# Transposing transfers out of SBUF and row factors by block transpose in a two-branch token mixer

## The chip, the cores and the metric

The kernel runs on one core of a Trainium2 chip. The metric is device time in microseconds (us) of one execution. TensorE (PE) multiplies matrices and can also transpose through an identity matrix; VectorE (DVE), ScalarE (ACT) and GpSimd (POOL) do elementwise work; SyncE (SP) issues nearly all transfers, in one queue, in program order. SBUF is the on-chip memory of 128 partitions, PSUM the accumulator memory that PE writes, DRAM the memory off the core.

## The reference, cut to what matters

S is 2048 rows, D is 512 columns, F is 1376; everything is bf16 in and out.

```python
xn = layernorm(x)                      # no gain or bias
# branch A: sliding dilated attention, 32 heads of 16, window of 8 rows 2 apart
q, k, v = split(xn @ wqkv)
o = softmax(q . k[s - 2*w]) . v[s - 2*w]   # per head, w = 0..7, masked before row 0
s = o @ wo
# branch B: shifted mixer and MLP on the same xn
h  = gelu(layernorm(xn) @ w1)          # a second layernorm of an already normed row
hs = [h0 one row later, h1 one row earlier, h2 two later, h3 two earlier] @ w2
x1 = xn + hs
h2 = gelu(layernorm(x1) @ w3) @ w4
out = x + s * silu(x1 + h2)
```

The second layernorm of a row that is already normed only multiplies it by a factor near one. This is the row factor below.

## The kernel before, in words

Rows are split into even rows (p = 0) and odd rows (p = 1), 1024 each, and these into four chunks of 512 rows: chunks 0 and 1 are even, 2 and 3 are odd. A chunk has four tiles of 128 rows. The order of the work is written out by hand: every instruction goes through `pin`, which keeps each engine's instructions in program order, and waits come from data dependencies alone. Transfers complete on eight counters in rotation, so that a transfer also waits for the one issued eight before it.

The first half of the program (to about 112 us) makes the operands, the second half (18 rounds of attention blocks, with the w4 products and the output products between them) uses them. In the first half, a chunk goes through these steps:

- `Norm.stats`, `root` and `apply` (L219 to L240) norm the rows in place in `xn`: statistics and apply on DVE, the root on POOL (on ACT for chunk 0).
- `turn` (L296) transposes two tiles on PE into a PSUM bank, and DVE copies them (L303) to `xnT`, the transposed rows. Chunk 0's first two tiles go one by one through `turn_one` (L307), which is copied out by ACT (L313).
- `rows2` (L248) makes the row factors, one column of 128 for each tile. The factors are needed along the free dimension, the same in all partitions. `rows2_spread` (L264, chunks 1 and 2) transposes them on PE (L266), copies them on DVE (L268), writes them to DRAM as `r2_d` (L269) and reads them back to all partitions into the last quarter of `xn2T` (L271). `rows2_here` (L273, chunks 0 and 3) spreads them with a product by ones on PE (L282) instead, copied out by ACT (L284) or DVE (L286).
- `scaled` (L288) multiplies `xnT` by the factors into `xn2T` on DVE.
- `q_all`, `k_all`, `v_pair` and `w1` multiply `xnT` or `xn2T` by weights on PE, each as halves of 8 products of 128x512. A half fills one bank of a pair of PSUM banks; there are three pairs in rotation (`pair`, L91). ACT empties them: q by L339, k twice by L354 (even and odd heads), v by L373, w1 by L400 with the gelu.
- `w2` (L415) multiplies the shifted rows of `hT`, DVE adds to `xn` (L435) and takes statistics; `columns` (L443) norms into `xn3`, writes the chunk to `x1n_dram` (L446) and reads it back transposed as `x1nT` by one transposing transfer of 512x512 (L450). `w3` (L459) multiplies it (L469) into `h3a` and `h3b`.

The values v are written to DRAM (`v_d`, L377) for the second half. The weights w3 and w4 are loaded at L545 and L574, between the steps of chunks 1 and 2. The part of the order that the change touches is, before:

```python
w1(0, 0); rows2_spread(1); load w3; turn(1, 0); turn(1, 1); w1(0, 1)
l2 stats, root, apply; rows2(2); l3 stats, root
scaled(1); q_all(1); k_all(1); v_pair(0, 4); l3.apply; rows2(3); v_pair(0, 6)
rows2_spread(2); w1(1, 0); turn(2, 0); turn(2, 1); w1(1, 1)
scaled(2); q_all(2); turn(3, 0); turn(3, 1); k_all(2); load w4
rows2_here(3); scaled(3); w1(2, 0); w1(2, 1); w1(3, 0); w1(3, 1); w2(0); columns(0)
```

Of the kernel before, what the change touches and what calls it, by code (L numbers as in the profile page):

```python
# [8 lines left out]
AF = mybir.ActivationFunctionType  # L9
ALU = mybir.AluOpType  # L10
BF16 = mybir.dt.bfloat16
# [3 lines left out]
def ap_of(base, dims, off=0):  # L15

    return bass.AP(base.tensor, base.offset + off, dims)
# [3 lines left out]
def kernel(  # L21
# [32 lines left out]
    CH = 512  # L54
    NCH = S // CH
    TPC = CH // P
# [22 lines left out]
    dram = ctx.enter_context(tc.tile_pool(name="dram", bufs=1, space=bass.MemoryType.DRAM))  # L79
# [8 lines left out]
    PS = psp.tile([P, 8, CH], F32, name="PS")  # L88
# [21 lines left out]
    wv_sb = b4([P, ND, D], "wv_sb")  # L110
    load_x(0, 0, 1)
    load_x(0, 1, 1)
    pin(SP.dma_start(out=wv_sb, in_=wqkv_v[:, :, 2 * D : 3 * D]))
    load_x(0, 2, 1)
    load_x(0, 3, 1)
    pin(SP.dma_start(out=wqk_sb[:, :, 0:D], in_=wqkv_v[:, :, 0:D]))
# [9 lines left out]
    w3_sb = wpl.tile([P, WS], BF16, name="w3_sb", tag="w")[:, 0 : ND * F].rearrange("p (dt f) -> p dt f", f=F)  # L126
# [11 lines left out]
    pin(DVE.memset(eps_t[:], EPS))  # L138

    for i in range(10):  # L140
        pin(PE.matmul(
            PS[:, 6 + i % 2, :], lhsT=ones_bf[:], rhs=ones_bf.unsqueeze(1).to_broadcast([P, TPC, P]),
            start=True, stop=True,
        ))

# [7 lines left out]
    m57 = const.tile([P, QB], BF16, name="m57")  # L153
    e_sb = const.tile([P, 8, 8, 16], BF16, name="e_sb")
    zero = const.tile([P, D], BF16, name="zero")

    def head_masks():
        pin(DVE.tensor_reduce(
# [36 lines left out]
    hT = [b8([P, ND, M + 2], f"hT{p}") for p in range(2)]  # L195
    kM = [kbp.tile([P, ND, MK, 2], BF16, name=f"kM{p}", tag="kM") for p in range(2)]
    v_d = [dram.tile([MK, 2, D], BF16, name=f"v_d{p}") for p in range(2)]
    r2_d = dram.tile([NCH, CH], BF16, name="r2_d")
    x1n_dram = dram.tile([S, D], BF16, name="x1n_dram")
    vst = [b4([P, 2, 2, D], f"vst{i}") for i in range(2)]  # L200


# [4 lines left out]
    def small_t(name, shape, dt=F32):  # L207
        return small.tile(shape, dt, name=name, tag=name)
# [37 lines left out]
    xn2Ts, r2s = {}, {}  # L246

    def rows2(c, ln):  # L248

        r2 = small_t("r2", [P, TPC])  # L250
        r2b = small_t("r2b", [P, TPC], BF16)
        eng = DVE if c == 0 else POOL
        pin(eng.tensor_tensor(out=r2, in0=ln.rstd, in1=ln.rstd, op=ALU.mult))
        pin(eng.tensor_tensor(out=r2, in0=r2, in1=ln.mv[:, :, 1], op=ALU.mult))
        if c == 0:
            pin(ACT.activation(r2, r2, AF.Sqrt, bias=eps_t[:]))
            with nc.allow_low_precision("bf16 row factors"):
                pin(DVE.reciprocal(out=r2b, in_=r2))
        else:
            rsqrt_eps(r2, r2)  # L260
            pin(POOL.tensor_copy(out=r2b, in_=r2))
        r2s[c] = r2b

    def rows2_spread(c):  # L264
        pt = single().bitcast(BF16)[0:TPC, 0:P]
        pin(PE.transpose(pt, r2s[c], ident[:]))  # L266
        t = small_t("r2t", [TPC, P], BF16)
        pin(DVE.tensor_copy(out=t, in_=pt))  # L268
        pin(SP.dma_start(out=r2_d[c].rearrange("(j q) -> j q", q=P), in_=t))  # L269
        xn2Ts[c] = b4([P, ND, CH], "xn2T")  # L270
        pin(SP.dma_start(out=xn2Ts[c][:, ND - 1, :], in_=r2_d[c : c + 1, :].to_broadcast([P, CH])))  # L271

    def rows2_here(c):  # L273
# [9 lines left out]
        if c == 0:  # L283
            pin(ACT.activation(t[:, ND - 1, :], pt, AF.Copy))  # L284
        else:
            pin(DVE.tensor_copy(out=t[:, ND - 1, :], in_=pt))  # L286

    def scaled(c):  # L288
        p, k = c // 2, c % 2
        t = xn2Ts[c]  # L290
        pin(DVE.tensor_tensor(
            out=t, in0=xnT[p][:, :, k * CH : (k + 1) * CH],
            in1=t[:, ND - 1, :].unsqueeze(1).to_broadcast([P, ND, CH]), op=ALU.mult,
        ))

    def turn(c, h):  # L296
        p, k = c // 2, c % 2
        i = k * TPC + 2 * h
        pt = single().bitcast(BF16).rearrange("p (a j q) -> p a j q", a=ND, j=2)
        for j in range(2):  # L300
            for dt in range(ND):
                pin(PE.transpose(pt[:, dt, j, :], xn[p][:, i + j, dt * P : (dt + 1) * P], ident[:]))  # L302
        pin(DVE.tensor_copy(  # L303
            out=xnT[p][:, :, i * P : (i + 2) * P], in_=pt.rearrange("p a j q -> p a (j q)")
        ))

    def turn_one(c, t):  # L307
        p, k = c // 2, c % 2
        i = k * TPC + t
        pt = single().bitcast(BF16)[:, 0 : ND * P].rearrange("p (a q) -> p a q", a=ND)  # L310
        for dt in range(ND):
            pin(PE.transpose(pt[:, dt, :], xn[p][:, i, dt * P : (dt + 1) * P], ident[:]))
        pin(ACT.activation(xnT[p][:, :, i * P : (i + 1) * P], pt, AF.Copy))  # L313

    def q_half(pts, lo, hi, nts=range(ND)):
        for nt in nts:
# [28 lines left out]
    def k_pad(p):  # L345
        pin(POOL.memset(kM[p][:, :, 0:8, :], 0.0))
        pin(POOL.memset(kM[p][:, :, M + 8 : MK, :], 0.0))

    def k_all(c, parts=(0, 1)):
        p, k = c // 2, c % 2  # L350
        for a in parts:
            pt = proj(c, a, wqk_sb[:, :, D : 2 * D], chunk(xnT, c))
            for e in range(2):
                pin(ACT.activation(  # L354
                    kM[p][:, 2 * a : 2 * a + 2, 8 + k * CH : 8 + (k + 1) * CH, e], pt, AF.Copy, scale=em[:, e : e + 1]
                ))
# [86 lines left out]
    def columns(c):  # L443
        ln = ln2[c]
        ln.apply(0, TPC)
        pin(SP.dma_start(  # L446
            out=x1n_dram[c * CH : (c + 1) * CH, :].rearrange("(i q) d -> q i d", q=P), in_=ln.dst
        ))
        x1nT = b4([P, ND, CH], "x1nT")
        pin(SP.dma_start_transpose(out=x1nT, in_=x1n_dram[c * CH : (c + 1) * CH, :]))  # L450
        x1nTs[c] = x1nT

    h3a, h3b = {}, {}
# [39 lines left out]
    pin(POOL.memset(zero, 0.0))  # L493
    k_pad(0)
    k_pad(1)
    pin(ACT.activation(
# [8 lines left out]
    for t in range(2):  # L505
        l0.root_act(t, t + 1, 1)
        l0.apply(t, t + 1)
    turn_one(0, 0)
    turn_one(0, 1)
    pv = pair()  # L510
    for t in range(2):
        v_mm(0, t, pv[:, t, :])
# [16 lines left out]
    for a in range(2):  # L529
# [10 lines left out]
    v_pair(0, 2)  # L540
    k_all(0, (1,))
    v_pad(0)
    w1(0, 0)
    rows2_spread(1)
    pin(SP.dma_start(out=w3_sb, in_=B_w3.rearrange("(dt q) f -> q dt f", q=P)))  # L545
    turn(1, 0)
    turn(1, 1)
    w1(0, 1)
    l2 = Norm(x_of(2), x_of(2), TPC, "l1")
    l2.stats(0, 4)  # L550
    l2.root()
    l2.apply(0, 4)
    rows2(2, l2)
    l3 = Norm(x_of(3), x_of(3), TPC, "l1")
    l3.stats(0, 4)
    l3.root()
    scaled(1)
    q_all(1)
    k_all(1)
    v_pair(0, 4)  # L560
    l3.apply(0, 4)
    rows2(3, l3)
    v_pair(0, 6)
    rows2_spread(2)
    w1(1, 0)
    turn(2, 0)
    turn(2, 1)
    w1(1, 1)
    scaled(2)
    q_all(2)  # L570
    turn(3, 0)
    turn(3, 1)
    k_all(2)
    pin(SP.dma_start(  # L574
        out=w4_sb[:, 0 : NF - 1, :],
        in_=B_w4[0 : (NF - 1) * P, :].rearrange("(ft q) n -> q ft n", q=P),
    ))
    pin(SP.dma_start(out=w4_sb[0:FL, NF - 1, :], in_=B_w4[(NF - 1) * P : F, :]))
    rows2_here(3)
    scaled(3)  # L580
    w1(2, 0)
    w1(2, 1)
    w1(3, 0)
    w1(3, 1)
    w2(0)
    columns(0)
    v_pad(1)
    q_all(3)
# [403 lines left out]
```

## Time and profile before

| what | us |
|---|---|
| median of 3 runs | 199.26 |
| lowest and highest of them | 197.72, 199.69 |
| the profiled execution's own time | 197.26 |
| its span, first to last instruction | 195.5 |
| PE busy in the span | 185.5 (95%) |
| ACT busy | 133.3 (68%) |
| DVE busy | 117.8 (60%) |
| POOL busy | 19.1 (10%) |
| mean granted TensorE clock | 0.996 |

The profile is of one execution. A group is the instructions of one line and engine on the same tiles, with their number, busy time and mean; the waits say what ended the idle time ahead of an instruction; the chain of waits is followed back from the last instruction and shows what set the end; the timeline lists instructions in order of time, merged where they follow each other, as start, length, engine, line, operation and number. PEld is the weight load ahead of a product, SPq the issue of a transfer on SP. A product of 128x512 is shown with 379 ns, and follows the one before it after some 216 ns, since products overlap.

### The profile page before, as it was taken

To read this page: it belongs to the slowest core of one execution; us is meant where nothing else is said; L and a number is where in the kernel's file an instruction comes from. 1 tells how busy PE (TensorE), PEld (TensorE's weight loads), DVE (VectorE), ACT (ScalarE), POOL (GpSimd) and SP (SyncE) were. 2 spreads that over 40 slices of the span, in tenths; PEclk is the share of its full clock that TensorE was granted. 3 is DMA by queue.
4 is the path that set the end of the run, shared out by engine and by line. 5 is a ranking of instruction groups with operands and counts; after the bars stand their busy time and mean duration, and the time that the engine had idled before them with its cause. 6 is when DMAs were issued, how large, how long until landed. Compare 5 with 4: busy or idle time off the path is not lost.

```text
span 195.5 us, 5255 instructions
## 1 busy us (share of the span) xinstructions
PE 185.5 (95%) x2253; PEld 91.8 (47%) x2283; DVE 117.8 (60%) x229; ACT 133.3 (68%) x151; POOL 19.1 (10%) x57
## 2 busy tenths in 40 slices
PE   7899999999999999999999999999999999999990
PEld 2474544554444444444444444445444544554540
DVE  5785767236076697494200035556487888798894
ACT  7399769649817615435656588877887876887871
POOL 3006066100002022006000000000000000000000
PEclk9999999999999999999999999999999999999998
DMA  4997480654000433752480051457565556582523
GB/s 131 339 368 239 132 282 15 218 158 157 0 0 3 136 83 109 215 107 65 110 260 0 0 162 60 157 166 232 153 216 161 137 155 215 127 247 51 171 91 126
DMA packets 33576, 28.12 MB, mean 144 GB/s; under 512 B 10760, under 2 KB 32528, under 8 KB 33552
## 3 DMA queue, kind: packets, MB, share of 16 engines
q1 hardware_dynamic: 33408, 27.71, 47.2%
q8 instruction: 18, 0.29, 0.6%
q10 hardware_dynamic: 144, 0.07, 0.1%
q14 instruction: 6, 0.05, 0.1%
HBM read 17.01 MB, written 8.67 MB: 131 GB/s over the span
## 4 chain that ended last, share of the span: by engine, by line
PE 85%; DMA 5%; DVE 4%; issue 2%; SPq 1%; ACT 1%
PE PS L469 19%; PE PS L328 19%; PE PS L764 19%; PE PS L427 5%; PE PS L811 4%; PE PS L795 4%; PE PS L652 3%; DMA wqk_sb<-in_A_wqkv_dram 3%; PE PS L626 3%; PE PS L362 3%; DMA x1nT<-x1n_dram 2%; PE PS L318 2%; PE PS L662 2%; PE PS L302 2%; DVE sg L825 2%
## 5 line engine op out<-in xcount | busy, mean ns | idle before, releaser
L469 PE MATMUL PS<-x1nT,w_sb 128*128 128x512 bf16 (+1 forms) x173 | 38.2, 379 | 0.4 <-DMA x1nT<-x1n_dram 0.3
L633 ACT ACTIVATE prob<-PS 128x1824 bf16<-128x1824 f32 x18 | 30.4, 1688 | 4.4 <-PE PS L626 3.6
L764 PE MATMUL PS<-w_sb,h3a 128*128 128x512 bf16 x112 | 29.2, 379 | 1.9 <-issue 1.7
L475 ACT ACTIVATE h3a<-PS 128x1024 bf16<-128x1024 f32 x16 | 16.4, 1024 | 21.0 <-PE PS L469 19.1
L777 DVE TENSOR_TENSOR xn<-PS,xn 128x512 bf16<-128x512 f32 x15 | 10.3, 686 | 32.0 <-PE PS L764 31.8
L469 PEld LDWEIGHTS <-w_sb 128*128 128x128 bf16 (+1 forms) x176 | 17.5, 100 | 20.9 <-issue 0.7
L328 PE MATMUL PS<-xnT,wqk_sb 128*128 128x512 bf16 x109 | 25.0, 379 | 0.2
L354 ACT ACTIVATE kM<-PS,em 128x1024 bf16<-128x1024 f32 x16 | 20.8, 1404 | 3.2 <-PE PS L328 3.2
L638 DVE TENSOR_TENSOR prob<-prob,maskb 128x1824 bf16<-128x1824 bf16 x18 | 19.8, 1102 | 1.8 <-ACT prob L633 1.8
L764 PEld LDWEIGHTS <-h3a 128*128 128x128 bf16 x128 | 11.3, 97 | 13.4 <-issue 1.2
L328 PEld LDWEIGHTS <-wqk_sb 128*128 128x128 bf16 x112 | 10.9, 98 | 12.8
L435 DVE TENSOR_TENSOR xn<-PS,xn 128x1024 bf16<-128x1024 f32 x8 | 9.6, 1213 | 11.3 <-PE PS L427 11.3
L811 PE MATMUL PS<-wo_sb,oT 128*128 128x512 bf16 (+1 forms) x68 | 15.5, 366 | 0.0
L328 PE MATMUL PS<-xn2T,w_sb 128*128 128x512 bf16 x62 | 14.6, 379 | 0.1
L427 PE MATMUL PS<-w_sb,hT 128*128 128x512 bf16 x63 | 14.4, 379 | 0.1
L821 ACT ACTIVATE sg<-PS 128x512 bf16<-128x512 f32 (+1 forms) x17 | 9.6, 572 | 6.1 <-PE PS L811 6.1
L764 PE MATMUL PS<-w_sb,h3b 128*128 128x512 bf16 (+1 forms) x44 | 12.8, 380 | 0.8 <-issue 0.8
L339 ACT ACTIVATE qT<-PS 128x1024 bf16<-128x1024 f32 x8 | 8.1, 1024 | 7.6 <-PE PS L328 7.6
L373 ACT ACTIVATE vst<-PS 128x512 bf16<-128x512 f32 (+1 forms) x12 | 8.8, 743 | 3.5 <-ACT sig L784 2.3
L221 DVE BATCH_NORM_STATS2 l1s<-xn 128x6 f32<-128x512 bf16 x16 | 10.1, 680 | 1.6 <-DMA xn<-in_A_x_dram 1.6
L400 ACT ACTIVATE hT<-PS 128x1024 bf16<-128x1024 f32 x8 | 8.1, 1031 | 3.8 <-PE PS L328 3.8
L221 DVE BATCH_NORM_STATS2 l3s<-xn 128x6 f32<-128x512 bf16 x16 | 10.2, 682 | 0.2
(105 smaller groups left out, 229.2 us busy)
## 6 DMA issues: line engine op xcount, KB each, us to landing
ring<-v_d SPq DMA_DIRECT2D x18, 256.0 KB, 3.3
v_d<-vst SPq DMA_DIRECT2D x16, 256.0 KB, 2.7
x1n_dram<-xn SPq DMA_DIRECT2D x4, 512.0 KB
xo<-in_A_x_dram SPq DMA_DIRECT2D x8, 256.0 KB, 4.1
ring<-rec_d SPq DMA_DIRECT2D x4, 456.0 KB, 4.7
out_dram<-xo SPq DMA_DIRECT2D x7, 256.0 KB
xn<-in_A_x_dram SPq DMA_DIRECT2D x6, 256.0 KB, 7.9
w_sb<-in_B_w_dram SPq DMA_DIRECT2D x1, 1376.0 KB
```

The source lines that it names most:

```text
L221: pin(DVE.bn_stats(out=self.st[:, j, :], in_=self.src[:, j, :]))
L328: pin(PE.matmul(pt[:, b, :], lhsT=w[:, dt, nt * P : (nt + 1) * P], rhs=rhs[:, dt, :], start=(dt == 0), stop=(dt == ND - 1),))
L354: pin(ACT.activation(kM[p][:, 2 * a : 2 * a + 2, 8 + k * CH : 8 + (k + 1) * CH, e], pt, AF.Copy, scale=em[:, e : e + 1]))
L427: pin(PE.matmul(pt[:, j, :], lhsT=w2_src(p, g, m0), rhs=w2_sb[:, g, :], start=(g == 0), stop=(g == ND - 1),))
L435: pin(DVE.tensor_tensor(out=xs, in0=pts[h], in1=xs, op=ALU.add))
L469: pin(PE.matmul(pt[:fs, ft % 2, :], lhsT=w3_sb[:, dt, ft * P : ft * P + fs], rhs=x1nT[:, dt, :], start=(dt == 0), stop=(dt == ND - 1),))
L475: pin(ACT.activation(t[:, o : o + 2, :], pt, AF.Gelu_apprx_tanh))
L633: pin(ACT.activation(pr, S_ps[:, :, 0 : ND * NQ], AF.Exp, scale=SCALE))
L638: pin(DVE.tensor_tensor(out=f, in0=f, in1=maskb[:], op=ALU.min))
L764: pin(PE.matmul(pt, lhsT=h3_of(c, ft)[:fs, jj * P : (jj + 1) * P], rhs=w4_sb[:fs, ft, :], start=(ft == 0), stop=(ft == NF - 1 and silu < 2),))
L777: pin(DVE.tensor_tensor(out=x_i, in0=pt, in1=x_i, op=ALU.add))
L811: pin(PE.matmul(pt[:, 0:W], lhsT=oT[p][:, dt, i * P : (i + 1) * P], rhs=wo["sb"][:, dt, c], start=(dt == 0), stop=(dt == ND - 1),))
```

## The change

Four things change.

1. Chunks 2 and 3 are no longer transposed on PE. `turn_dma` issues four transposing transfers on SP, one for each tile of 128x512, from `xn` straight to `xnT`, both in SBUF. Likewise `columns` no longer writes to DRAM and reads back: it issues four transposing transfers from `xn3` to `x1nT`.
2. Row factors of chunks 1 to 3 are cast by POOL into a zeroed tile of 32 columns for each chunk (`r2p`); DVE's block transpose turns it in blocks of 32x32, and one transfer with runs of 32 numbers puts it into `r2_d`. `rows2_spread` falls into `rows2_write` and `rows2_read`, which stand apart in the order; chunk 3 uses them too, so `rows2_here` is left for chunk 0 alone.
3. At the start, wv is loaded in two halves, DVE instead of ACT copies the first tile's transposes, and the last of the ten warm-up products has half its width.
4. The order: transfers of chunk 2 and 3 right behind their norms, the load of w3 behind all row factors and just ahead of w4, and `w2(0)` ahead of `w1(3, 1)`.

```diff
-    pin(SP.dma_start(out=wv_sb, in_=wqkv_v[:, :, 2 * D : 3 * D]))
+    for h in range(2):
+        pin(SP.dma_start(
+            out=wv_sb[:, 2 * h : 2 * h + 2, :], in_=wqkv_v[:, 2 * h : 2 * h + 2, 2 * D : 3 * D]
+        ))
...
     for i in range(10):
+        w = TPC if i < 9 else 2
...
+            r2b = r2p[:, c, :]
+            pin(POOL.tensor_copy(out=r2b[:, 0:TPC], in_=r2))
...
-    def rows2_spread(c):
-        pt = single().bitcast(BF16)[0:TPC, 0:P]
-        pin(PE.transpose(pt, r2s[c], ident[:]))
-        t = small_t("r2t", [TPC, P], BF16)
-        pin(DVE.tensor_copy(out=t, in_=pt))
-        pin(SP.dma_start(out=r2_d[c].rearrange("(j q) -> j q", q=P), in_=t))
+    def rows2_write(c):
+        t = small_t("r2t", [P, 32], BF16)
+        pin(DVE.transpose(out=t, in_=r2s[c]))
+        pin(SP.dma_start(out=ap_of(r2_d[c], [[32, P // 32], [P, 32], [1, 32]]), in_=t))
+
+    def rows2_read(c):
         xn2Ts[c] = b4([P, ND, CH], "xn2T")
-        pin(SP.dma_start(out=xn2Ts[c][:, ND - 1, :], in_=r2_d[c : c + 1, :].to_broadcast([P, CH])))
+        pin(SP.dma_start(out=xn2Ts[c][:, ND - 1, :], in_=r2_d[c : c + 1, 0:CH].to_broadcast([P, CH])))
...
-    def turn_one(c, t):
+    def turn_one(c, t, eng):
...
-        pin(ACT.activation(xnT[p][:, :, i * P : (i + 1) * P], pt, AF.Copy))
+        dst = xnT[p][:, :, i * P : (i + 1) * P]
+        pin(DVE.tensor_copy(out=dst, in_=pt) if eng is DVE else ACT.activation(dst, pt, AF.Copy))
+
+    def turn_dma(c):
+        p, k = c // 2, c % 2
+        for t in range(TPC):
+            i = k * TPC + t
+            pin(SP.dma_start_transpose(out=xnT[p][:, :, i * P : (i + 1) * P], in_=xn[p][:, i, :]))
...
-        pin(SP.dma_start(
-            out=x1n_dram[c * CH : (c + 1) * CH, :].rearrange("(i q) d -> q i d", q=P), in_=ln.dst
-        ))
         x1nT = b4([P, ND, CH], "x1nT")
-        pin(SP.dma_start_transpose(out=x1nT, in_=x1n_dram[c * CH : (c + 1) * CH, :]))
+        for t in range(TPC):
+            pin(SP.dma_start_transpose(out=x1nT[:, :, t * P : (t + 1) * P], in_=ln.dst[:, t, :]))
...
-    turn_one(0, 0)
-    turn_one(0, 1)
+    turn_one(0, 0, DVE)
+    turn_one(0, 1, ACT)
...
+    rows2_write(1)
     w1(0, 0)
-    rows2_spread(1)
-    pin(SP.dma_start(out=w3_sb, in_=B_w3.rearrange("(dt q) f -> q dt f", q=P)))
     turn(1, 0)
     turn(1, 1)
+    rows2_read(1)
     w1(0, 1)
...
     l2.apply(0, 4)
+    turn_dma(2)
     rows2(2, l2)
...
     l3.root()
+    rows2_write(2)
     scaled(1)
     q_all(1)
     k_all(1)
+    l3.apply(0, 4)
+    turn_dma(3)
+    rows2_read(2)
+    rows2(3, l3)
+    rows2_write(3)
     v_pair(0, 4)
-    l3.apply(0, 4)
-    rows2(3, l3)
     v_pair(0, 6)
-    rows2_spread(2)
+    rows2_read(3)
+    pin(SP.dma_start(out=w3_sb, in_=B_w3.rearrange("(dt q) f -> q dt f", q=P)))
     w1(1, 0)
-    turn(2, 0)
-    turn(2, 1)
     w1(1, 1)
     scaled(2)
     q_all(2)
-    turn(3, 0)
-    turn(3, 1)
     k_all(2)
+    scaled(3)
...
-    rows2_here(3)
-    scaled(3)
     w1(2, 0)
     w1(2, 1)
     w1(3, 0)
+    w2(0)
     w1(3, 1)
-    w2(0)
     columns(0)
```

More of the change, by code (lines that the diff above doesn't have):

```diff
@@ L140 @@
     for i in range(10):
+        w = TPC if i < 9 else 2
         pin(PE.matmul(
-            PS[:, 6 + i % 2, :], lhsT=ones_bf[:], rhs=ones_bf.unsqueeze(1).to_broadcast([P, TPC, P]),
+            PS[:, 6 + i % 2, 0 : w * P], lhsT=ones_bf[:], rhs=ones_bf.unsqueeze(1).to_broadcast([P, w, P]),
             start=True, stop=True,
@@ L155 @@
     zero = const.tile([P, D], BF16, name="zero")
+    r2p = const.tile([P, NCH, 32], BF16, name="r2p")
     def head_masks():
@@ L197 @@
     v_d = [dram.tile([MK, 2, D], BF16, name=f"v_d{p}") for p in range(2)]
-    r2_d = dram.tile([NCH, CH], BF16, name="r2_d")
-    x1n_dram = dram.tile([S, D], BF16, name="x1n_dram")
+    r2_d = dram.tile([NCH, 32 * P], BF16, name="r2_d")
     vst = [b4([P, 2, 2, D], f"vst{i}") for i in range(2)]
@@ L250, in rows2 @@
         r2 = small_t("r2", [P, TPC])
-        r2b = small_t("r2b", [P, TPC], BF16)
         eng = DVE if c == 0 else POOL
@@ L256, in rows2 @@
             pin(ACT.activation(r2, r2, AF.Sqrt, bias=eps_t[:]))
+            r2b = small_t("r2b", [P, TPC], BF16)
             with nc.allow_low_precision("bf16 row factors"):
@@ L260, in rows2 @@
             rsqrt_eps(r2, r2)
-            pin(POOL.tensor_copy(out=r2b, in_=r2))
+            r2b = r2p[:, c, :]
+            pin(POOL.tensor_copy(out=r2b[:, 0:TPC], in_=r2))
         r2s[c] = r2b
-    def rows2_spread(c):
-        pt = single().bitcast(BF16)[0:TPC, 0:P]
-        pin(PE.transpose(pt, r2s[c], ident[:]))
-        t = small_t("r2t", [TPC, P], BF16)
-        pin(DVE.tensor_copy(out=t, in_=pt))
-        pin(SP.dma_start(out=r2_d[c].rearrange("(j q) -> j q", q=P), in_=t))
+    def rows2_write(c):
[3 more added lines that the diff above has]
+    def rows2_read(c):
         xn2Ts[c] = b4([P, ND, CH], "xn2T")
-        pin(SP.dma_start(out=xn2Ts[c][:, ND - 1, :], in_=r2_d[c : c + 1, :].to_broadcast([P, CH])))
+        pin(SP.dma_start(out=xn2Ts[c][:, ND - 1, :], in_=r2_d[c : c + 1, 0:CH].to_broadcast([P, CH])))
     def rows2_here(c):
@@ L282, in rows2_here @@
         pin(PE.matmul(pt, lhsT=ones_bf[:], rhs=t[:, 0, :], start=True, stop=True))
[L283 to L286, printed above, removed]
+        pin(ACT.activation(t[:, ND - 1, :], pt, AF.Copy))
     def scaled(c):
@@ L493 @@
     pin(POOL.memset(zero, 0.0))
+    pin(POOL.memset(r2p, 0.0))
     k_pad(0)
```

## The prediction

> **What bounds the kernel now.** I read the page's busy row first, then the chain of waits, then the timeline around each edited line. PE is busy 95% of the span, and the chain of waits is PE on nearly every step; so what counts is PE time removed, and whether anything else then holds PE up. The chain of waits in order of time (start, length, what) names the steps that the change touches:
>
> ```profile
> 3.21 5.68 DMA wqk_sb<-in_A_wqkv_dram
> ...
> 35.46 0.89 PE PS L302 x16
> 36.36 4.53 PE PS L328 x21
> ...
> 41.54 0.89 PE PS L302 x16
> ...
> 66.16 4.51 DMA x1nT<-x1n_dram
> 70.80 0.81 PE PS L469 x3
> ```
>
> The two L302 pieces are the transposes of chunks 2 and 3, on the path. The first line says that the start hangs on wqk's landing, the last two that w3(0) hangs on x1nT's. The timeline around chunks 1 to 3 gives the lengths (start, length, engine, line):
>
> ```profile
> 28.34 5.16 ACT L354 ACTIVATE kM<-PS,em 128x1024 bf16<-128x1024 f32 x4 [0.70 <-PE PS L328]
> 29.87 3.62 PE L362 MATMUL PS<-wv_sb,xnT 128*128 128x512 bf16 x15
> 33.56 1.90 PE L328 MATMUL PS<-xn2T,w_sb 128*128 128x512 bf16 x8
> 36.19 1.89 PE L328 MATMUL PS<-xn2T,w_sb 128*128 128x512 bf16 x8
> 42.27 3.62 PE L328 MATMUL PS<-xnT,wqk_sb 128*128 128x512 bf16 x16
> 44.20 5.17 ACT L354 ACTIVATE kM<-PS,em 128x1024 bf16<-128x1024 f32 x4 [1.60 <-PE PS L328]
> 45.94 7.09 PE L328 MATMUL PS<-xn2T,w_sb 128*128 128x512 bf16 x31
> ```
>
> Sixteen products take 3.62 us to the last one's end, and the next may start 0.16 earlier: 3.46 for a q, k or v stage, 1.73 for a half. ACT's 5.2 us for a k stage is longer than PE's 3.46.
>
> **PE work removed.** w1(1,0) starts at 33.56 and w1(1,1) at 36.19: 2.63 less 1.73 leaves 0.90 for turn(2). q_all(2) starts at 37.92, k_all(2) at 42.27: 4.35 less 3.46 leaves 0.89 for turn(3). w1(0,0) starts at 18.36, w1(0,1) at 21.23: 2.87 less 1.73 less 0.90 for turn(1), which stays, leaves 0.24 for L266 of chunk 1. L266 of chunk 2 (0.22 at 33.41) gains nothing: w1(1,0) needs the pair of banks that ACT empties at 28.34 + 5.16 = 33.50, and starts 0.06 later. L282 of chunk 3 delays w1(2,0) by 3.67 less 3.46 = 0.21, but w1(3,0), at 45.94 + 3.46 = 49.40, needs the bank that ACT empties at 44.20 + 5.17 = 49.37; so this also gains nothing. Sum 0.90 + 0.89 + 0.24 = **2.03 us**. DVE loses 4 L303 copies of 0.69, one L286, one L277, none of them on the path.
>
> **w2(0) ahead of w1(3,1).** PE does the same work. w2(0) needs the banks and the gelu of w1(2,0), w1(2,1). In the new time (2.03 earlier, k_all(2) from 40.2) ACT empties k until 47.3 and these two until 49.4; w1(3,0) runs 47.4 to 49.1, w2(0) 49.1 to 52.5, its second half from 50.8. It fits by 0.7 us or more. DVE's adds then start at 51.0 instead of 54.86, and columns(0) applies from 58.1 instead of 61.76.
>
> **x1nT.** PE ends w2(2) at 63.23 + 7.31 = 70.54 and starts w3(0) at 70.80: **0.27 us** goes if x1nT is there. Its write and read took from 63.17 to 70.7; the four transfers start at 58.5, and w3(0) is due at 68.5. For chunks 1 to 3, w3 follows the apply by 10 us or more, so nothing there is late unless four transfers take that long.
>
> **The price of a transposing transfer out of SBUF (T, for 128x512)** is what no row shows. The nearest is the transfer out of DRAM, four times the size:
>
> ```profile
> L450 SPq DMA_TRANSPOSE x1nT<-x1n_dram x4: 1308/1980/2202, 66.2 to 94.9; - x4
> ```
>
> Below, T is a quarter of the shortest, 0.33; above, the whole 2.2, if the cost is the instruction's and not its size's. Plain issues cost 0.24 to 0.55 on SP whatever their size, so I take 0.4 fixed and a quarter of the other 1.6: **T = 0.8 us**, landing 2.4 after issue as at 68.36 to 70.7. The queue on SP is now: four T of chunk 2 (from 26.41 + 0.41 = 26.8), write of factors 2, four T of chunk 3 (from 33.2, behind l3.apply at 32.81), read 2, write 3, four v_d writes (34.40 for 2.52 before), read 3, w3, w4. With T = 0.8 chunk 2 lands at 32.4, q_all(2) is due at 36.8. Read 2 is issued at 36.5 and takes 3.1 (39.26 to 42.37 before), scaled(2) 1.23, so xn2T is there at 40.8 and w1(2,0) due at 43.7: 2.9 us to spare. Read 3, behind the v_d writes, goes out near 39.7: done at 44.0, due at 47.4. w3 and w4 (2.7 MB; 28 to 30 and 44 to 46 moved 240 to 356 GB/s) are in by 50, due at 68. All hidden: 0. The cover is gone at T = 1.5: chunk 3 then goes out until 39.2, and w1(2,0) waits for every bit more, fourfold to 1.6 and eightfold beyond, where chunk 2's tail holds up chunk 3. The block transpose on DVE is 128x32, bounded by 0.06 (the smallest memset) and 0.21 (L268), and stands where L268 did; the smaller runs of r2_d make its write up to some us longer than 1.3 (21.19 to 22.48), against 5 us to spare for scaled(1).
>
> The Trainium skill speaks against this change (VectorE: DVE Perf Modes, The three transpose paths): it gives 1309 ns for a 128x128 transpose by DMA and 390 ns on TensorE. By it T would be an estimated 5.2 us and the total near 227; the trace has 16 blocks landed in 4.5 us, 0.28 a block, and PE's 16 in 0.89, so I do not use it in the sum.
>
> **The start.** wv's second issue puts wqk's 0.43 later on SP (L113's 0.43). wqk lands behind 1 MB of x and wv that has moved only at about 6.0 (184 GB/s from 2 to 4 us, 338 from 4 to 6), 2.4 after even the later issue: 0, at worst 0.43. DVE's copy lets v start about 0.3 earlier, but PE idles 0.28 ahead of q_half for wqk already: 0 again, and the shorter warm-up, at most 0.2, falls in the same idle time.
>
> **Sum:** 2.03 + 0.27 = 2.3 us off. The profiled execution would take 197.26 - 2.3 = 195.0; it is 2.0 below the median shown, and runs are compared by medians, so I forecast 199.26 - 2.3 = **197.0**, own range 196.0 to 198.2.
>
> **The rivals.** (a) Slower: SP is the new bound. If T is the whole 2.2 of the row, four for chunk 2 go out until 35.6, chunk 3 until 44.8, read 2 at 45.1; scaled(2) ends at 49.4 where w1(2,0) is due at 43.7: 5.7 late, net +3.4, 202.7. It decides from T = 1.8, where the 2.3 is used up. For it: 2.2 was measured, and 24 transposing issues stand on the queue instead of 4. Against: it takes none of the 2.2 to be for size.
> (b) One transfer at a time: each waits the 4.5 us from issue to landing of the row, so read 2 goes at 26.8 + 36 + 0.7 = 63.5, and w1(2,0) is 24 late: 221. This is close to what the figure of the Trainium skill above (VectorE: DVE Perf Modes, The three transpose paths) comes to. Against it: 16 blocks overlap in the row, and eight counters let eight transfers fly.
> (c) Given back, within 1%: ACT, whose k stages already set w1(1,0) and w1(3,0), takes one of the two turns (0.9), and wqk the 0.43: 2.3 less 1.33, 198.3; or T near 1.7, read 2 at 41.1 and w1(2,0) 1.7 late: 198.7. For it: ACT has 16.4 us of work in the 19.2 from 28.1 to 47.3. Against: outside those two places its banks are free 1 us ahead.
> (d) More: the start gains the 0.28 of its wait and loses bandwidth to nothing, and shorter queues later save another 0.7: 196.0 or less; nothing in the trace asks for it.
>
> **How the numbers follow.** About 1% is what a measurement of this kernel can tell from no change: 197.3 and 201.3. Forecast 0.58, of which 0.39 lies under 197.3; (d) 0.06; (c) 0.17, of which 0.15 within 1% and 0.02 above; (a) 0.16; (b) 0.03. Faster 0.45, same 0.34, slower 0.21. The range reaches from the sum on the profiled execution's own scale, which also covers most of (d), to (a): 195.0 to 202.8.
>
> **What would show it.** Right: no L302 after 22 us on PE, w1(1,1) 1.73 behind w1(1,0), q_all(2) and k_all(2) without a gap, w3(0) starting near 68.5 without a wait for x1nT, and a transposing issue under 1.5 us. Wrong: DVE's scaled(2) or PE's w1(2,0) waiting on xn2T, or q_all(2) on xnT, or issues of 2 us; or q_half starting after 9.0.

## The result: 1% slower, inside the range, on the other side

| | changed kernel | kernel before, on the same chip |
|---|---|---|
| median, us (20 runs each) | 199.96 | 197.74 |
| lowest and highest, us | 198.58, 203.68 | 196.43, 200.14 |
| profiled execution, us | 198.7 | 197.26 (the one of the prediction) |
| its span, us | 197.0 | 195.5 |

The ratio is 1.0099, 95% interval [1.0075, 1.0122]: slower by 1%, and the interval does not reach 1. Forecast were 197.0 us and 2.3 us off; 199.96 lies in the range of 195.0 to 202.8, but the sign is wrong. Ratios and intervals in this document leave out executions that took over 1.5% more than the fastest of their kernel.

The PE timeline shows where the two kernels part (start of the stage, us):

| stage | before | after | after less before |
|---|---|---|---|
| q_half, first product | 8.94 | 9.14 | +0.20 |
| w1(1,0) | 33.56 | 33.51 | -0.05 |
| w1(2,0) | 45.94 | 43.86 | -2.08 |
| q_all(3) | 56.32 | 56.26 | -0.06 |
| w3(0) | 70.80 | 70.31 | -0.49 |
| first w4 product | 112.24 | 111.75 | -0.49 |
| end of the span | 195.5 | 197.0 | +1.5 |

The forecast 2 us were there at w1(2,0), were lost again within 12 us, and another 2 us were lost from the first w4 product on, where the change touches no code. The first loss stands in the timeline of the changed kernel around chunks 2 and 3 (start, length, engine, line, operation, number, idle time before and what ended it):

```profile
26.79 5.22 SPq L323 DMA_TRANSPOSE xnT<-xn  x4
...
33.28 5.13 SPq L323 DMA_TRANSPOSE xnT<-xn  x4
33.51 3.61 PE L338 MATMUL PS<-xn2T,w_sb 128*128 128x512 bf16 x16
36.95 7.07 PE L338 MATMUL PS<-xnT,wqk_sb 128*128 128x512 bf16 x32
38.50 0.53 SPq L277 DMA_DIRECT2D xn2T<-r_d  x1
39.13 0.53 SPq L273 DMA_DIRECT2D r_d<-r2t  x1
39.76 2.81 SPq L387 DMA_DIRECT2D v_d<-vst  x4
...
42.66 0.56 SPq L277 DMA_DIRECT2D xn2T<-r_d  x1
...
43.86 3.62 PE L338 MATMUL PS<-xn2T,w_sb 128*128 128x512 bf16 x16
...
48.06 1.23 DVE L294 TENSOR_TENSOR xn2T<-xnT,xn2T 128x2048 bf16<-128x2048 bf16 x1 [4.66 <-DMA xn2T<-r_d]
49.34 1.90 PE L338 MATMUL PS<-xn2T,w_sb 128*128 128x512 bf16 x8 [1.87 <-DVE xn2T L294]
```

PE runs without a gap from w1(1,0) to the end of w1(2,1): no transposes, q_all(2) and k_all(2) in one piece of 32 products. Then w1(3,0) waits 1.87 us for scaled(3), and scaled(3) for read 3, which SP issued at 42.66 behind the four v_d writes, and which took 5.28 us to land. The chain of waits in order of time (start, length, what) has the same read in it, and two new entries in the second half:

```profile
3.70 5.40 DMA wqk_sb<-in_A_wqkv_dram
...
42.66 5.28 DMA xn2T<-r_d
...
139.59 5.63 DMA v_d<-vst
...
159.85 0.63 issue
```

The first line is the start: wqk's issue is now at 3.70 instead of 3.21. "issue" is time in which PE waited for nothing that the profile shows. The PE timeline has it at two places (start, length, and so on as above, the idle time and its releaser last):

```profile
143.22 0.39 PE L662 MATMUL PS<-prob,ring 128*32 128x57 bf16 x28
144.26 0.21 PE L662 MATMUL PS<-prob,ring 128*32 128x57 bf16 x4 [0.65 <-issue]
...
159.54 0.32 PE L672 MATMUL PS<-prob,den_st 128*32 128x114 bf16 x10
160.49 0.28 PE L672 MATMUL PS<-prob,den_st 128*32 128x114 bf16 x6 [0.63 <-issue]
```

PE stops in the middle of a run of value products that read the same tiles as the ones just done. Before, the products at the first of these places run through, and at the second there is a stop of 0.11 us, at 158.51 in its chain:

```profile
143.70 0.42 PE L652 MATMUL PS<-prob,ring 128*32 128x57 bf16 x32
...
158.22 0.72 PE L652 MATMUL PS<-prob,ring 128*32 128x57 bf16 x32
158.75 0.40 PE L662 MATMUL PS<-prob,den_st 128*32 128x114 bf16 x16
```

The price of a transposing issue, which the prediction could only bound, is a row now (the count, then shortest, median and longest in ns):

```profile
L323 SPq DMA_TRANSPOSE xnT<-xn x8: 1196/1218/1302, 26.8 to 37.2; - x8
```

The sixteen of `columns` (L458) have 1189, 1214 and 1270.

### The profile page after: what moved, and what is told of

The parts are those of the page before. It is cut to its first block, busy times and chain, and to the rows that moved or that the text cites. A ratio compares the mean times of both kernels' runs of the same rounds, so it can differ in the third digit from the quotient of the medians.

```text
span 197.0 us, 5263 instructions
## 1 busy us (share of the span) xinstructions
PE 187.0 (95%) x2248; PEld 90.2 (46%) x2248; DVE 114.9 (58%) x225; ACT 132.6 (67%) x150; POOL 19.3 (10%) x58
## 3 DMA queue, kind: packets, MB, share of 16 engines
q1 hardware_dynamic: 36572, 26.82, 47.4%
## 4 chain that ended last, share of the span: by engine, by line
PE 76%; DMA 8%; ACT 6%; DVE 5%; SPq 2%; issue 1%; ACTq 0%; DVEq 0%
PE PS L477 19%; PE PS L774 17%; PE PS L338 15%; PE PS L437 5%; PE PS L821 4%; PE PS L805 3%; DMA v_d<-vst 3%; PE PS L636 3%; DMA wqk_sb<-in_A_wqkv_dram 3%; DMA xn2T<-r_d 3%; PE PS L662 3%; PE PS L372 3%; ACT kM L364 3%; PE PS L328 2%; DVE xo L841 2%; PE PS L672 2%
## 5 line engine op out<-in xcount | busy, mean ns | idle before, releaser
L774 PE MATMUL PS<-w_sb,h3a 128*128 128x512 bf16 x128 | 32.7, 380 | 0.1
L445 DVE TENSOR_TENSOR xn<-PS,xn 128x1024 bf16<-128x1024 f32 x8 | 9.6, 1214 | 9.6 <-PE PS L437 9.6
L774 PE MATMUL PS<-w_sb,h3b 128*128 128x512 bf16 (+1 forms) x48 | 13.5, 381 | 0.0
L294 DVE TENSOR_TENSOR xn2T<-xnT,xn2T 128x2048 bf16<-128x2048 bf16 x4 | 4.8, 1206 | 11.5 <-DMA v_d<-vst 6.9
```

The source lines that it names most:

```text
L445: pin(DVE.tensor_tensor(out=xs, in0=pts[h], in1=xs, op=ALU.add))
L774: pin(PE.matmul(pt, lhsT=h3_of(c, ft)[:fs, jj * P : (jj + 1) * P], rhs=w4_sb[:fs, ft, :], start=(ft == 0), stop=(ft == NF - 1 and silu < 2),))
```

## The experiments

Two questions are open: what held read 3, and what costs 2 us in a second half that is the same code. "Second half" below is from the first w4 product to the end of the span: 83.3 us before, 85.25 after.

**Again, without an edit.** Is the second half's loss an accident of one execution?

> The changed kernel once more, for a second trace. In the first, PE reached w3(0) 0.49 us earlier than before (70.31 against 70.80) and the end 1.5 us later, so the second half lost 2.0 us, 1.5 of it between 138 and 151 us, where the read of the reciprocals (ring from rec_d) went out 5.1 us after its writes instead of 3.5. Theory H (the second half really is slower in this program): again w3(0) near 70.3, again a gap of 4.5 us or more between the first rec_d write and its read, span 197 or more. Rival J (an accident of one execution): w3(0) near 70.3 and the span 195.0, with a gap of 3.5 us.

Measured: 200.36 us, ratio 1.0136 [1.0094, 1.0178]. Second half 112.06 to 198.3, 86.2 us; the two stops of PE are there again, at the same products, with 1.30 and 1.37 us. The first read of reciprocals went out 4.5 us behind its first write. w1(3,0) waited 1.73 us. So both losses belong to the kernel, and Theory H holds.

**Read 3 ahead of the v_d writes.** The copies of v stay where they are, and their four transfers are issued behind the read:

```diff
-    v_pair(0, 4)
-    v_pair(0, 6)
+    late_v = []
+    v_pair(0, 4, late_v)
+    v_pair(0, 6, late_v)
     rows2_read(3)
+    for put in late_v:
+        put()
```

> The changed kernel with the four v_d writes of v_pair(0,4) and v_pair(0,6) issued behind the read of chunk 3's factors instead of ahead of it. Theory F (that read, 42.66 to 47.94 us, is late because it stands behind 1 MB of v_d writes): it goes out near 41.3 and lands near 44, the wait of 1.87 us ahead of w1(3,0) goes to 0, w3(0) starts near 68.5, and the time is 1.8 us lower than that of the changed kernel. Rival K (the read itself takes 5 us, for instance because 128 partitions read one row, or because w3 and w4 follow it): it lands at 46 or later, and at least 0.7 us of the wait stays. By H the second half still takes 85 us from the first w4 product to the end, by J 83.

Measured: 198.08 us, ratio 1.0018 [0.9992, 1.0044], 2.3 us less than the changed kernel beside it. The timeline of this kernel:

```profile
41.39 0.33 SPq L277 DMA_DIRECT2D xn2T<-r_d  x1
...
41.77 2.59 SPq L387 DMA_DIRECT2D v_d<-vst  x4
43.82 5.59 PE L338 MATMUL PS<-xn2T,w_sb 128*128 128x512 bf16 x24
...
44.41 1.23 DVE L294 TENSOR_TENSOR xn2T<-xnT,xn2T 128x2048 bf16<-128x2048 bf16 x1 [1.47 <-DMA xn2T<-r_d]
...
68.48 3.83 PE L477 MATMUL PS<-x1nT,w_sb 128*128 128x512 bf16 x17
```

The read goes out 1.3 us earlier and takes 3.0 us instead of 5.3, since the v_d writes no longer move ahead of it. w1(2,0) to w1(3,0) are 24 products in one piece, and w3(0) starts at 68.48, where the prediction put it (68.5). The first loss is this read's place, and Rival K is out. But the second half takes 86.1 us (109.92 to 196.0), with stops of 1.46 and 0.75 us, so all that the first half gains is lost there.

**Only the x1nT transfers, and only the start.** Two kernels with one part of the change each, on the kernel before. The first replaces the write to DRAM and the transposing read by four transposing transfers out of SBUF in `columns`; the second has wv in halves, DVE's copy and the shorter warm-up.

```diff
-        pin(SP.dma_start(
-            out=x1n_dram[c * CH : (c + 1) * CH, :].rearrange("(i q) d -> q i d", q=P), in_=ln.dst
-        ))
         x1nT = b4([P, ND, CH], "x1nT")
-        pin(SP.dma_start_transpose(out=x1nT, in_=x1n_dram[c * CH : (c + 1) * CH, :]))
+        for t in range(TPC):
+            pin(SP.dma_start_transpose(out=x1nT[:, :, t * P : (t + 1) * P], in_=ln.dst[:, t, :]))
```

```diff
-    pin(SP.dma_start(out=wv_sb, in_=wqkv_v[:, :, 2 * D : 3 * D]))
+    for h in range(2):
+        pin(SP.dma_start(
+            out=wv_sb[:, 2 * h : 2 * h + 2, :], in_=wqkv_v[:, 2 * h : 2 * h + 2, 2 * D : 3 * D]
+        ))
...
-    turn_one(0, 0)
-    turn_one(0, 1)
+    turn_one(0, 0, DVE)
+    turn_one(0, 1, ACT)
```

> The kernel before with one part of the change: x1nT by four transposing transfers out of SBUF for each chunk, without the copy in DRAM. Four issues of 1.2 us take 5 us where one write and one read took 7.5 from issue to landing, so x1nT(0) is there about 68, the wait of 0.27 us ahead of w3(0) goes, and the first half gains 0.2 to 0.3. Theory H2 (the second half loses because of what this part changes there: the DRAM tile that is gone, or the number of instructions on SP): the time rises by 1 to 2 us. Rival: the time falls by 0.3 or stays, and the second half takes 83 us.

> The kernel before with the start's edits alone: wv in halves, DVE's copy of the first tile, the last warm-up product half as wide. In the changed kernel q_half started at 9.14 instead of 8.94. If that belongs to these edits (one more issue of 0.47 us ahead of wqk on SP), it is 9.14 here too, and everything to 112 us is 0.2 later. If it was chance, 8.94. In the second half nothing of these edits is left; a loss of more than 0.5 us there would mean that the second half depends on the moment or on the instruction count at which it starts.

Measured: the x1nT transfers alone 196.60 us, ratio 0.9960 [0.9929, 0.9992]; no wait for x1nT, second half 83.1 us. The first w4 product comes 0.14 us earlier, less than the 0.2 to 0.3 expected. The start alone 198.69 us, ratio 1.0037 [1.0006, 1.0067]; q_half starts at 9.61 instead of 8.94, and the first w4 product is 1.24 us late. The chain of waits of the start alone says why q_half is late:

```profile
3.69 5.88 DMA wqk_sb<-in_A_wqkv_dram
...
9.61 1.05 PE PS L323 x8
```

So the x1nT edit pays, the start edits cost, and neither brings the second half's loss: 83.1 and 83.7 us, though the start alone shows one stop of 0.50 us, at 160.27. What is left is the turn of chunks 2 and 3 with the row factors. They change no instruction of the second half, but they shorten TensorE's program: 35 products fewer, of two instructions each (weight load and multiply), and 11 waits more. Counted in the compiled programs it has 4593 instructions before and with the start alone, 4600 with the x1nT transfers alone, 4534 after and 4535 with read 3 first.

**The place in the program.** Both stops of the changed kernel fall where the compiled program's count is 194 above a multiple of 256: instructions 2498 and 3266. To move the places without touching anything behind the warm-up, the warm-up products are made more and narrower:

```diff
-    for i in range(10):
-        w = TPC if i < 9 else 2
+    for i in range(33):
+        pin(PE.matmul(PS[0:32, 6 + i % 2, 0:16], lhsT=ones_bf[:, 0:32], rhs=ones_bf[:, 0:16], start=True, stop=True))
+    for i in range(6):
         pin(PE.matmul(
-            PS[:, 6 + i % 2, 0 : w * P], lhsT=ones_bf[:], rhs=ones_bf.unsqueeze(1).to_broadcast([P, w, P]),
+            PS[:, 6 + i % 2, :], lhsT=ones_bf[:], rhs=ones_bf.unsqueeze(1).to_broadcast([P, TPC, P]),
```

The second kernel below has no padding and the start edits of the diff above taken back; the third has both; the fourth is the kernel before with more of the padding:

```diff
-    for i in range(10):
+    for i in range(106):
+        pin(PE.matmul(PS[0:32, 6 + i % 2, 0:16], lhsT=ones_bf[:, 0:32], rhs=ones_bf[:, 0:16], start=True, stop=True))
+    for i in range(3):
```

> The changed kernel with the factor read of chunk 3 ahead of the v_d writes, and with its ten warm-up products made 39 (33 of them 16 columns wide), so that TensorE's program has 4593 instructions, as before the change, in place of 4535. Nothing behind the warm-up is different. Theory S1 (the stalls of 0.7 to 1.5 us that TensorE shows with no releaser at 143 and 159 us come at instructions whose place in the program is 194 more than a multiple of 256, and the change moved these places into the value products): the two stalls are gone or below 0.4 us, and from the first w4 product to the end of the span it takes 83.5 to 84.5 us instead of 86.1; the time is 195.5 to 197 (ratio 0.99 to 0.996). Theory S2 (the loss comes from the load of wo, issued 1.2 us late, and the transfers that it then meets): the stalls and the 86 us stay, and the ratio is 1.00.

> The same kernel with the start of before: wv in one transfer, ScalarE's copy of both first transposes, ten full warm-up products. TensorE's program keeps 4535 instructions; SyncE's has one transfer less ahead of the load of wo. The start edits were seen to cost 0.2 to 0.65 us at the first q product (9.11 and 9.6 against 8.94 and 8.99): expected 0.2 to 0.6 us earlier, the first q product at 8.9 to 9.0. S1: the two stalls at the value products stay, from first w4 product to end 85.5 to 86.2 us; ratio 0.996 to 1.0. S2, in the form that SyncE's own program has a place at which an issue takes 1.2 us more: that place now falls on the v_d write behind the load of wo, whose issue is back at 0.4 us, the factor read of the first round is issued 3.6 us behind its write instead of 5.3, and the second half is 84 us; ratio 0.985 to 0.99.

> Both edits together: read of chunk 3 first, the start of before, 39 warm-up products with TensorE's program again at 4593 instructions. If S1 and the cost of the start are both right: no stall over 0.4 us at the value products, first w4 product at 109.6, end of the span near 193.5; ratio 0.980 to 0.988, faster than both kernels. If S1 is wrong, as the run with the old start alone.

> The kernel before with 109 warm-up products (three full, 106 of 16 columns) in place of ten, so that TensorE's program has 4791 instructions: 198 more, which puts its places of 194 above a multiple of 256 where the changed kernel with the read first has them. Nothing else is different; the start may lose up to 1 us if the narrow products take longer than the full ones that they stand for. S1: stalls of 0.5 us and more with no releaser appear at the value products near 145 and 160 us, and from first w4 product to end it takes 84.5 to 86 us instead of 83.1; slower by 1 to 3 us. S2: no stalls, 83.1 to 83.5 us, slower only by what the start loses.

| kernel | instructions | median, us | ratio and interval | first q_half | second half | stops of PE, us |
|---|---|---|---|---|---|---|
| read 3 first, padded | 4593 | 196.07 | 0.9896 [0.9859, 0.9933] | 9.77 | 83.4 | 0.43 |
| read 3 first, old start | 4535 | 197.26 | 0.9961 [0.9932, 0.9989] | 8.77 | 87.5 | 1.56, 0.93 |
| read 3 first, old start, padded | 4593 | 195.25 | 0.9883 [0.9840, 0.9927] | 9.14 | 84.85 | 1.01 |
| before, padded by 198 | 4791 | 201.32 | 1.0164 [1.0128, 1.0200] | 9.25 | 86.2 | 0.96, 0.33, 0.27 |

The places decide it, in both directions. 58 more instructions in the warm-up take 2.7 us out of the second half of one kernel; 198 more put 2.9 us into the kernel before, whose code from the transposes on is untouched, at the products where the changed kernel stops. These are single traces, but the medians agree: the 58 instructions take 2.0 us off in both pairs of kernels (198.08 to 196.07, 197.26 to 195.25). Nor is it the moment at which the second half starts: read 3 first begins it at 109.92 and takes 86.1 us, a padded kernel further below at 110.00 and takes 83.3. The PE timeline of the kernel before, padded:

```profile
146.11 0.22 PE L654 MATMUL PS<-prob,ring 128*32 128x57 bf16 x5 [0.96 <-issue]
...
161.32 0.28 PE L664 MATMUL PS<-prob,den_st 128*32 128x114 bf16 x6 [0.33 <-issue]
```

What is fetched at these places can be seen. The queues of the kernel with read 3 first, in the half microsecond from 140.5 us (packets, MB, share of 16 engines):

```profile
q1 hardware_dynamic: 140, 0.14, 107.0%
q8 instruction: 1, 0.02, 11.7%
```

Queue q8 moves one packet of 16 KB for every 256 instructions of PE (17 packets with 4535 instructions, 18 with 4593). This one starts at 140.8, at a time at which q1 keeps the engines full, and PE goes on at 143.23; the next packet that counts is at 157.0, and PE goes on at 159.47. In the changed kernel and its repeat PE goes on some 2.3 us behind such a packet as well (one that starts between 141.5 and 142, and 144.26; between 142.5 and 143, and 145.22). The Trainium skill (Runtime: NRT & Kernel Launch, Instruction fetch mechanics) says that the instructions come in blocks of 16 KiB, 256 of them, fetched while the block before is executed, and that crossing a boundary is mostly hidden. The size of the blocks is the trace's; hidden it is not, where it costs 0.4 to 1.6 us.

How a stop comes about can be timed in the five traces that hold a record of every PE product (the changed kernel twice, read 3 first, x1nT alone, start alone). There is one packet for each such place, and it starts about when PE passes the place before, from 2.0 us ahead of that to 3.5 us behind it. In the seven stops of the second half PE goes on 2.29 to 2.53 us behind the start of the packet (2.4 to 2.8 in the other kernels); at the 55 other places it arrives 2.79 us or more behind it and doesn't stop. In the seven, the packet also starts late, 1.5 to 3.5 us behind the place before, and the share of q1 in that time is 81 to 112%.

Not every such place costs. The stops of 0.4 us and more came where the place lies behind 90 to 150 short instructions of scores and values in a row, in the second round after a read of factors from DRAM was issued. Before, instruction 2754 lies behind 130 of them, one round later, and PE shows no stop there. That traffic holds the packet up is argued from these rows; no run changed the traffic alone. Nor does the same place always cost the same: with 4593 instructions the one near 158 us gave 0.11 us before, 0.50 with the start alone, 0.43 and 1.01 in the two padded kernels, and none with wv whole (below).

With old start and padding, 1.01 us of stop was left at 157.26, more than the 0.4 expected, and the ratio of 0.9883 is just above the 0.980 to 0.988 expected. With the old start alone the second half is longer than expected (87.5 us against 85.5 to 86.2). The form of the rival in which SP's own program delays the load of wo is wrong: with one transfer less ahead of it the issue still took 1.30 us.

**A better place, and three controls.** A count of 4667, 74 more than before, puts the two places behind w4 products and to the head of the scores, in the kernel with read 3 first and the old start (71 narrow and five full warm-up products) and in the kernel before (41 and six). Another kernel only pads the changed kernel (33 and six), and the last is the first padded one with wv whole again:

```diff
-    for h in range(2):
-        pin(SP.dma_start(
-            out=wv_sb[:, 2 * h : 2 * h + 2, :], in_=wqkv_v[:, 2 * h : 2 * h + 2, 2 * D : 3 * D]
-        ))
+    pin(SP.dma_start(out=wv_sb, in_=wqkv_v[:, :, 2 * D : 3 * D]))
```

> The changed kernel as it is, and only its ten warm-up products made 39 (33 of 16 columns, six full), so that TensorE's program has 4592 instructions, one less than before the change. The wait of w1(3,0) for the factor of chunk 3 stays (1.7 to 1.9 us). If the places in TensorE's program are all of the second half's loss: from first w4 product to end 83.1 to 84.2 us in place of 85.3 and 86.2, the time 196.3 to 197.9, ratio 0.992 to 1.0, where the changed kernel had 1.010 and 1.014. If the read with its wait, or the transfers, also slow the second half: 85 us and a ratio of 1.005 or more.

> The kernel with the read of chunk 3 first and the start of before, with 76 warm-up products (71 of 16 columns, five full): 4667 instructions, 74 more than before the change. The places of 194 above a multiple of 256 then fall behind the w4 products (2498) and 17 instructions into the scores that follow w4 products (3266), in place of the end of the scores and the value products. If the stall is long where many quick products stand ahead of such a place while the factors of a batch are read: no stall with no releaser over 0.2 us at 142 and 157 us, against 1.01 at 157 in the run with 4593 instructions; end of the span 193.0 to 194.2, time 194.0 to 195.2, ratio 0.980 to 0.987. If it only moves: a stall of 0.4 to 1.2 us elsewhere, ratio 0.987 to 0.992.

> The kernel before, with 47 warm-up products (41 of 16 columns, six full), 4667 instructions too. It had one stall of 0.23 us (0.62 in the run with the start edits alone) at its value products, so this place gives it 0.2 to 0.6 us at most, less what the start loses by the narrow products: ratio 0.996 to 1.001. Whatever it is, the difference between this and the kernel of the same placing is what the transposing transfers are worth: by the forecast 1.9 to 2.3 us. If the placing alone makes the gain, both come out alike.

> The kernel with the read of chunk 3 first and 4593 instructions, with VectorE's copy and the shorter warm-up kept, but wv in one transfer as before. If the second issue of wv is what delays wqk: its first issue is back at 3.2 us (3.7 with halves), the first q product starts at 8.8 to 9.2 us and the wait for wqk is 0.4 to 0.8 us (9.77 and 1.42 us with halves), ratio 0.985 to 0.990 against 0.990. If VectorE's copy delays it: 9.4 us or later.

| kernel | median, us | ratio and interval | first q_half | first w4 product | second half | stops of PE, us |
|---|---|---|---|---|---|---|
| changed kernel, padded | 201.05 | 1.0122 [1.0021, 1.0223] | 9.77 | 113.78 | 83.1 | none |
| read 3 first, old start, placed | 195.36 | 0.9878 [0.9813, 0.9943] | 9.09 | 110.11 | 83.5 | none |
| before, placed | 198.94 | 1.0071 [1.0035, 1.0106] | 10.03 | 115.12 | 83.5 | 0.31 |
| read 3 first, wv whole, padded | 195.74 | 0.9894 [0.9820, 0.9967] | 8.97 | 110.00 | 83.3 | none |

The placed kernel runs through where the others stop. Its PE timeline:

```profile
141.15 0.40 PE L636 MATMUL PS<-qT,kM 32*128 32x57 bf16 x32
141.48 0.42 PE L662 MATMUL PS<-prob,ring 128*32 128x57 bf16 x32
141.73 0.39 PE L672 MATMUL PS<-prob,den_st 128*32 128x114 bf16 x16
142.27 1.46 PE L774 MATMUL PS<-w_sb,h3a 128*128 128x512 bf16 x6 [0.16 <-issue]
```

Its four executions lie between 195.17 and 195.78 us, at 0.988 of the kernel before, just above the 0.980 to 0.987 expected, and in time as good as 195.25 above; the two have the lowest medians, but the intervals of all four kernels with read 3 first and moved places overlap. wv whole puts wqk's first issue back to 3.22 and q_half at 8.97, with VectorE's copy kept: in these traces it is the second issue of wv that delays q_half, not the copy. The wait for wqk is still 0.95 us, above the 0.4 to 0.8 expected, and the ratio (0.9894 against 0.9896) shows no gain from it.

Two controls did not come out as expected. The changed kernel with padding alone has the second half mended (83.1 us, no stop) and is no faster: its first half got 2.0 us worse. The timeline of it:

```profile
33.92 6.09 SPq L324 DMA_TRANSPOSE xnT<-xn  x4
...
44.04 0.62 SPq L278 DMA_DIRECT2D xn2T<-r_d  x1
...
51.38 1.90 PE L339 MATMUL PS<-xn2T,w_sb 128*128 128x512 bf16 x8 [3.06 <-DVE xn2T L295]
```

An instruction packet now starts in the half microsecond from 36.5, inside the four transposing issues, and they take 6.09 instead of 5.13 us; together with q_half's 0.63 that puts read 3 1.4 us later, and it lands 6.0 us after its issue. So a wait without slack in the first half takes up what is won in the second. The profiled execution is the shortest of this kernel (198.64 against a median of 201.05); where the others lost another 2 us, no trace shows. The kernel before with 74 instructions more lost 2.9 us ahead of the first w4 product. Its q_half starts at 10.03, because six of the v products ahead of it take 2.76 us instead of some 1.5 (why is open), and the factor product of chunk 3 waits 1.44 us for VectorE, which is held up by read 2. The profiled execution is also the longest of its ten (200.37 against a median of 198.94). So it doesn't tell what the placing alone is worth to it, nor, as was planned, what the transposing transfers are worth at equal places. Its second half, 83.5 us, says that there is little to win there: before, the places lie well as it is.

## Why the prediction was wrong

- **PE work removed: right.** Between w1(1,0) and w1(2,0) the kernels take 12.38 and 10.35 us: 2.03, of which 0.90 and 0.89 are the two turns and 0.21 is L282 of chunk 3, which I had given no gain. That the forecast sum is also 2.03 is luck: its third term was another one. The 0.24 of L266 in chunk 1 shows as 0.05 at w1(1,0), since the start ate 0.20. With read 3 in place and the start repaired, the first w4 product comes at 109.56 without padding and at 110.00 to 110.15 with it, 2.7 and 2.1 to 2.2 us ahead of before, against 2.3 forecast.
- **x1nT: right.** The wait of 0.27 at w3(0) is gone in every kernel with the four transfers; alone they are worth 0.4% (interval 0.1 to 0.7), which holds the 0.27.
- **T = 0.8 us was too low, but inside its bounds.** An issue takes 1.2 us, four of them 5.2. The plain issues that it was built from are not all 0.24 to 0.55 either: in the same timeline w4's took 0.86 (at 39.65) and the four v_d writes 0.63 each. T stays under the 1.5 at which the prediction saw the cover gone, and no product waited for xnT. By the figure of the Trainium skill that spoke against the change (VectorE: DVE Perf Modes, The three transpose paths: 1309 ns for a block of 128x128) T would have been an estimated 5.2. In the trace a transfer of four such blocks goes out every 1.3 us. Rivals (a) and (b) are out.
- **The step that failed first: "Read 3, behind the v_d writes, goes out near 39.7: done at 44.0, due at 47.4. All hidden: 0."** Two terms of it were too small. It went out at 42.66, 3.0 late: 2.0 of that is T (the four issues for chunk 3 end at 38.41 instead of 36.4), the rest the two small issues and the v_d writes, 4.2 us together instead of 3.3. And it landed in 5.28 us, behind 1 MB of v_d issued just ahead of it, not in the 3.1 of read 2 before, where those writes had ended their issue 2.3 us earlier; issued ahead of them it took 3.0. scaled(3) ended at 49.3, the due time was 47.4, and the 1.87 us between are PE's wait. The spare of 2.9 us that I gave to scaled(2) was down to 0.4. I worked out what T = 1.5 does to read 2 and w1(2,0) and left read 3 at the one value; the tightest consumer was the one behind the most transfers.
- **The start: 0, at worst 0.43, was wrong on the low side.** It cost 0.2 in the profile of the changed kernel, 0.65 in its repeat and 0.67 alone. I had argued from the bytes ahead of it that wqk's landing absorbs the later issue; it doesn't: with wv whole and the issue at 3.22, q_half started at 8.97, with halves and 3.69 at 9.77. A q_half after 9.0 was one of the prediction's own signs of being wrong.
- **The step that is not in the prediction at all: the second half.** I took the code from w3 on as unchanged and its time as fixed. Its instructions are the same, but 59 places earlier in the program, and that costs some 2 us by the medians, 2 to 4 in single traces. In the five traces whose second half takes 85 us or more, PE's stops are 1.3 to 2.7 us of it. The rest is not split up: in these traces, and only there, the issue of wo's load takes 1.3 to 1.75 us instead of 0.4, the factors of the first batch are read 4.1 to 5.3 us behind their write instead of 3.0 to 3.8, and in two of them a v_d write that ACT waits for lands after 5.6 us (139.59 in the chain above) and 6.2 us (read 3 first, at 137.88). All of it comes and goes with the padding, so the places are shown as the cause (a stop of 1.01 us was left in one padded kernel); which share goes through wo was not tested apart.
- **(c), given back within 1%,** is the nearest rival by its time (198.3 to 198.7), but neither its size nor its way is right: it still had the kernel 0.6 to 1.0 us faster, by ACT and wqk. The loss came by one read and the places of instruction blocks.
- **The base was 1.5 us high.** 199.26 was the median of three runs; 20 runs of the kernel before have 197.74. The change is therefore 2.2 us slower, not 0.7. That 199.96 lies in the range is luck: the range reaches that far for rival (a), which did not happen.

## What to carry to other kernels

When transfers are added to a queue, follow each small read behind them to its consumer, with the landing time that it has behind a megabyte and not alone; put reads that a product waits for ahead of writes that nobody waits for. When a change takes instructions out of TensorE's program, look at stages that the change doesn't touch: a loss with "issue" as its releaser, in the middle of short products, moves with the program's length, and some 30 to 70 tiny products at the start can move it away (here the first q product came 0.3 us later for it, or more). Before a change is called a loss, its parts are worth separating: here two of three pay, and without the start edits, with one transfer moved and the program's places put right, the change is 1.2% faster than the kernel before (0.9878 [0.9813, 0.9943]). What the move of w2(0) and the block transpose are worth was not tested apart.

## What the runs showed of the hardware

- PE's program comes in packets of 16 KB, one for 256 instructions. Where PE reaches the next place before some 2.3 to 2.8 us have passed since the start of the packet, it stops for the rest, up to 1.56 us here. That took a quick stretch and a packet that started late.
- An instruction packet also delays transfers that SP issues at that moment. After 100 us, the fourteen traces have 49 issues of over 1 us on SP; a packet starts within 0.5 us of the start of 48 of them, and of 105 of the 680 shorter ones. The load of wo at 128.69 took 1.56 us with a packet in the half microsecond from 128.5; before, the same issue took 0.41 and three others took long, at 137.77 (1.58), 144.61 (1.62) and 148.42 (1.28), with packets from 137.5, 144.5 and 148.0. Padding PE's program, with SP's left as it is, moved wo's issue from 1.74 to 0.44 (read 3 first) and from 0.41 to 1.57 (before). A packet from 134.0 before, beside the two writes of rec_d, did nothing that shows.
- One stop of 1.56 us was followed by a lower granted clock. The kernel with read 3 first and the old start, in two stretches of PE (window, length, busy time and instructions, granted clock, DMA share, GB/s):

```profile
140.00:144.00 4.00, 2.28 (x86) 0.96 0.41 137
144.00:148.00 4.00, 4.00 (x20) 0.62 0.45 135
```

  The products after the stop follow each other in about 0.43 us instead of 0.22 for some 3 us, which makes this second half the longest, 87.5 us. The Trainium skill (TensorE: Matmul & The Clock Gate, Why this matters for your kernels) has the clock drop after a gap of some 3 us; here 1.56 us came ahead of it, in one execution.
- DVE's block transpose of 128x32 took 0.18 to 0.21 us, and a transposing transfer of 128x512 from SBUF to SBUF 1.2 us of SP.
